# Declared waits of GpSimd operations behind VectorE ones in the paired stage

## The chip, the cores and the metric

The kernel runs on one core of a Trainium2 chip. A core has TensorE (PE in the profile: matrix products into the PSUM banks), VectorE (DVE), ScalarE (ACT), GpSimd (POOL) and SyncE (SP, which issues DMAs). Each works through its own list of instructions in order, and semaphores tie the lists together. The metric is the device time of one execution in microseconds (us), the median of several runs.

## What is computed

Windowed attention with a distance bias, followed by a dense mixture of four experts. All arrays are float32.

```python
# attention: 4 batches, 8 heads, 576 positions, 64 wide; window 128
scores = scale * np.matmul(q, k.transpose(0, 1, 3, 2))
scores = np.where(mask, scores + bias[None], -1000000000.0)   # bias: -slope * distance
attn = np.exp(scores - max); attn = attn / (sum + 1e-09)
attn_out = np.matmul(attn, v)
# experts: x is attn_out as 2304 rows of 512; w1 is 4 x 512 x 1024, w2 is 4 x 1024 x 512
p = domain_probs / (domain_probs.sum(-1, keepdims=True) + 1e-09)
for e in range(E):
    h = np.maximum(x @ w1[e], 0.0)
    out += p[:, e:e + 1] * (h @ w2[e])
```

## The kernel before

Each float32 factor is held as two fp32r numbers, a rounded one (`xh`, `w2h`, `rh`: "high") and the rest (`xl`, `w2l`, `rl`: "low"). A product is made of three matmuls: high x high, high x low, low x high. To split a value is a `cast` (L338 on ScalarE or L340 on VectorE) and then a `minus` (L360 on VectorE or GpSimd), which subtracts the high part from the value.

The 2304 rows stand in seven blocks, the hidden layer in 16 units of 256 columns (four to an expert). For the last blocks, 5 and 6 (384 rows each), units 4 to 15 run two at a time: `pair` (L1329), six pairs, the last 200 us of the kernel. Both layers are done there with seven products of half-size blocks in place of eight, which needs sums and differences of the factors. The first layer is `sevenfold` (matmuls L1236), seven products for each of the two units, called a and b. The second layer is `multiply` (matmuls L1469), products named "12", "22", "11", 1, 2, 3 and 4, each in two parts. Each product is added onto a PSUM bank, and VectorE adds it, weighted with `prob`, into the output tile `acc` (`weighted`, L1488). That is the eviction: a product that adds onto a bank again waits for it. Product 11 and then product 2 use the same two banks.

Products 1 to 4 need four sums S1 to S4 of rectified results, each in two halves of columns (`fi` 0 and 1). `joined` (L1384) and `plus` (L1090) make the raw sums; in the traces they are `w1r` (S1 in one buffer, S2 in the other) and `q` (S3 and S4). `split` (L1396) splits them: S1, S2 and S4 into `xh` and `xl`, S3 into `rh` and `rl`. S4's raw sum is `q<-k,w1r`; S2's is `w1r<-q,k`. Where GpSimd does a `minus` or `plus`, `pieces` (L346) cuts it in two instructions if it has 384 elements or more.

Products 2, 3, 22 and 4 of one pair run among the first-layer products of the next one (the list `rest`): after the first a product comes product 2, part 0, then a, then 2, part 1, and so on. The weights of the pair stage are split already and parked in DRAM; `unparked` (L993) loads them by four DMAs a pair that GpSimd issues. `mixed` (L1021) makes the sums of the second-layer weights (`w2r`, `v`, `acc` to `w2h`, `w2l`, and into `xh`, `xl`).

Nothing is ordered by hand. Each operation is an `Op` with the engines it may run on, a time by which it is due and the keys it reads and writes; `Plan.order` (L88) places one after the other with estimated durations, picks the engine, and the program is emitted in the order of the planned starts. An operation that names VectorE or GpSimd in `port` is kept from overlapping, in the plan, with others that name it. In the program only the data dependencies are enforced, by semaphores; what the plan keeps apart may overlap when the engines run off its times.

Of the kernel before, what the change touches and what calls it, by code (L numbers as in the profile page):

```python
# [11 lines left out]
AF = mybir.ActivationFunctionType  # L12
ALU = mybir.AluOpType
# [7 lines left out]
def f(ap):  # L21
    return ap.bitcast(F32)
# [13 lines left out]


class Op:
    __slots__ = ("n", "engs", "emit", "due", "deps", "outs", "wait", "ready", "bufs", "cold", "start", "end", "eng", "port", "late", "lag")


class Plan:
# [7 lines left out]
    }  # L50

    def __init__(self):
        self.ops, self.last, self.readers, self.places = [], {}, {}, {}

    def op(self, engs, emit, due, reads=(), writes=(), holds=(), cold=None, port=None, late=0.0, lag=0.0):

        o = Op()
        o.n, o.engs, o.emit, o.due = len(self.ops), dict(engs), emit, due
        o.deps, o.outs, o.bufs, o.start = set(), [], [], None


        o.port, o.late, o.lag = (POOL,) if port is None else port, late, lag
        o.cold = 2 * o.engs.get(PE, 0.0) if cold is None else cold
        for key in reads:
            if key in self.last:
                o.deps.add(self.last[key])
        for key in writes:
            if key in self.last:
                o.deps.add(self.last[key])
            o.deps.update(self.readers.get(key, ()))  # L70
        o.deps.discard(o)
        for key in reads:
            self.readers.setdefault(key, []).append(o)
        for key in writes:
            self.last[key] = o
            self.readers[key] = []
        for key in (*reads, *writes, *holds):
            b = key[0] if isinstance(key, tuple) else key
            b = getattr(b, "buf", b)
            if isinstance(b, Buf) and b not in o.bufs:  # L80
                o.bufs.append(b)
                b.uses += 1
        for d in o.deps:
            d.outs.append(o)
        self.ops.append(o)
        return o

    def order(self):  # L88
        at = dict.fromkeys((PE, DVE, ACT, POOL, SP), 0.8)
        queue = {e: [] for e in at}  # L90
        bus = port = 0.0
        landed = [0.0] * FLIGHT
        owner = {tag: [None] * len(p) for tag, p in self.places.items()}

        def push(o):
            o.ready = {e: max((d.end + (EXTRA if d.eng != e or e != PE else 0.0) + self.GAP[d.eng][e] for d in o.deps), default=0.0) + o.late for e in o.engs}
            for e in o.engs:
                queue[e].append(o)

        def slots(o):  # L100

            t, taken = -1.0, []
            for b in o.bufs:
                if b.place is not None:
                    continue
                best = None
                for i, w in enumerate(owner[b.tag]):
                    if (b.tag, i) in taken or (w is not None and w.done < w.uses):
                        continue
                    free = w.free if w is not None else -1.0  # L110
                    if best is None or free < best[0]:
                        best = (free, i)
                if best is None:
                    return None
                t = max(t, best[0])
                taken.append((b.tag, best[1]))
            return t, taken

        for o in self.ops:
            o.wait = len(o.deps)  # L120
            if not o.wait:
                push(o)
        out = []
        while len(out) < len(self.ops):
            best = None
            for e, q in queue.items():
                cands, least = [], None
                for o in q:
                    s = slots(o)
                    if s is None:  # L130
                        continue
                    t = max(at[e], o.ready[e], s[0] + 0.2 if s[1] else 0.0)
                    if e in o.port:
                        t = max(t, port)
                    if e == SP:
                        t = max(t, landed[-FLIGHT])
                    cands.append((t, o, s[1]))
                    least = t if least is None else min(least, t)
                if least is None:
                    continue  # L140
                t, o, taken = min(
                    (c for c in cands if c[0] <= least + SLACK), key=lambda c: (c[1].due, c[1].n)
                )

                key = (t, o.due, o.n)
                if len(o.engs) > 1:
                    end = t + o.engs[e]
                    if any(max(at[x], o.ready[x]) + d < end - 1e-6 for x, d in o.engs.items() if x != e):
                        key = (t + 0.3, o.due, o.n)
                        alt = [c for c in cands if len(c[1].engs) == 1 and c[0] <= least + SLACK]  # L150
                        if alt:
                            t, o, taken = min(alt, key=lambda c: (c[1].due, c[1].n))
                            key = (t, o.due, o.n)
                if best is None or key < best[0]:
                    best = (key, t, e, o, taken)
            assert best is not None, "the plan is stuck"
            _, t, e, o, taken = best
            for x in o.engs:
                queue[x].remove(o)
            o.eng, o.start = e, t  # L160
            if e == SP:
                at[e] = t + 0.5
                bus = max(bus, t + 1.2) + o.engs[e] / DBW
                o.end = bus + 0.85
                landed.append(o.end)
            else:
                o.end = t + (o.cold if e == PE and t < WARM else o.engs[e])
                at[e] = o.end
                if e in o.port:
                    port = o.end  # L170
                o.end += o.lag
            new = [b for b in o.bufs if b.place is None]
            for b, (tag, i) in zip(new, taken):
                owner[tag][i] = b
                b.place = self.places[tag][i]
            for b in o.bufs:
                b.done += 1
                b.free = max(b.free, o.end)
            for x in o.outs:
                x.wait -= 1  # L180
                if not x.wait:
                    push(x)
            out.append(o)
        return sorted(out, key=lambda o: (o.start, o.n))


DBW = 2.4e5
# [2 lines left out]
PLAIN = 4.0  # L190
FLIGHT = 9
SLACK = 0.1
EXTRA = 0.03
LATE_S = 1.79
LATE_T = 1.48
# [49 lines left out]
def attention_moe(  # L245
# [87 lines left out]
    def cast(o, i, n, due, reads, writes, sbuf=True):  # L333


        def emit(e):
            if e == ACT:
                nc.scalar.activation(o(), i(), AF.Copy)  # L338
            else:
                nc.vector.tensor_copy(o(), i())  # L340

        plan.op(
            {ACT: act(n) + (0.035 if sbuf else 0.0), DVE: dve2(n) if sbuf else dve(n)}, emit, due, reads, writes, port=(DVE,) if sbuf else ()
# [8 lines left out]
        at_ = (slice(None),) * axis  # L352
        return [[x[(*at_, slice(i * m, i * m + m))] for x in aps] for i in range(2)]

    def minus(o, a, b, n, due, reads, writes, gp=True):


        def emit(e):
            for x, y, z in pieces(e, n, o(), a(), b()):
                by[e].tensor_tensor(out=x, in0=y, in1=f(z), op=ALU.subtract)  # L360

        engs = {DVE: dve(n), POOL: pooled(n)} if gp else {DVE: dve(n)}
        plan.op(engs, emit, due, reads, writes, port=(DVE, POOL) if gp else ())

# [719 lines left out]

    def plus(o, a, b, n, due, reads, writes, op=ALU.add):
        def emit(e):
            for x, y, z in pieces(e, n, o(), a(), b()):
                by[e].tensor_tensor(out=x, in0=y, in1=z, op=op)  # L1090

        plan.op({DVE: dve(n), POOL: pooled(n)}, emit, due, reads, writes, port=(DVE, POOL))

# [234 lines left out]

    def pair(l0, l1, due, between):  # L1329

        w0 = wst[l0]
        nbs = joint[l0]
        n = BLOCKS[nbs[0]][1]
# [57 lines left out]
        def halves(name, fi, src, keys, d, sbuf, free=()):  # L1391
            h, lo, hk, lk = R[name, fi]
            relu(h, src, [*keys, *free], hk, d)
            joined(lo, src, h, ALU.subtract, [*keys, hk], lk, d, sbuf)

        def split(i, fi):  # L1396
            h, lo, hk, lk = S[i, fi]
            r_, rk = s_raw(i, fi), s_key(i, fi)
            n0 = len(plan.ops)
            cast(h, r_, n, ready[i], [rk], [hk])  # L1400
            minus(lo, r_, h, n, ready[i], [rk, hk], [lk], i > 2)
            if i < 3:
                after_group(n0)

# [12 lines left out]
        def result1(src, keys, fi, b):  # L1417
# [9 lines left out]
            if len(hold) == 1 and (b == 1) == (fi == 0):  # L1427
# [2 lines left out]
                joined(s_raw(3, fi), src, raw(a21, fi), sub, [*keys, key(a21, fi)], s_key(3, fi), d, False)  # L1430
                plus(s_raw(2, fi), s_raw(3, fi), raw(a22, fi), n, ready[2] - 0.5, [key(a22, fi), s_key(3, fi)], [s_key(2, fi)], sub)
                plus(s_raw(4, fi), raw(a12, fi), s_raw(2, fi), n, ready[4] - 0.5, [key(a12, fi), s_key(2, fi)], [s_key(4, fi)])
                split(3, fi)
                if fi:
                    split(2, 0)
                    split(2, 1)

        spare = Buf("av")
        s0, at0, _ = sevenfold(l0, due, result0, Part(spare, lambda t: t.place[0], 0))
# [248 lines left out]
    outs = []  # L1688
# [37 lines left out]
            outs = [] if l in pairs else [(l, b, i) for b in (nb if l in joint else [nb]) for i in range(BLOCKS[b][1] // P)]  # L1726

    with tc.manual_schedule():
        for o in plan.order():
            o.emit(o.eng)  # L1730


MARGIN = 15.32
# [65 lines left out]
```

## Time and profile before

| | us |
|---|---|
| median of 3 runs | 911.28 (911.26 to 913.27) |
| profiled execution | 911.12 |
| its span, first to last instruction | 909.1 |
| TensorE busy | 883.8 (97%) |
| VectorE busy | 739.5 (81%) |
| ScalarE busy | 474.6 (52%) |
| GpSimd busy | 462.0 (51%) |
| mean granted clock of TensorE | 0.991 |

The profile comes from one execution, and its times are counted from the start of the span. An engine's busy time holds no waiting for semaphores, but an instruction that has begun and is held up counts in full. In a timeline a bracket gives the idle time of the engine before the instruction, and who released it. Matmuls overlap with the one before: a row's duration is longer than the distance to the next.

### The profile page before, as it was taken

The numbers are of one execution on the slowest core, as the hardware profiler recorded it, in microseconds if no ns is written. First come the engines' busy times: TensorE is split into PE (matmuls) and PEld (weight loads), VectorE is DVE, ScalarE is ACT, GpSimd is POOL, SyncE is SP. The second block draws the span as 40 slices with busy tenths as digits, with TensorE's granted clock in tenths as the row PEclk, the third lists the DMA queues.
The fourth block names the chain that finished last, engine by engine and source line by source line (L and its number), as shares of the span: only waits on it lengthen the run. The fifth ranks groups of instructions, "written<-read, shape, count | busy, mean of one in ns | idle before, by whom it ended". The sixth has DMA issues, their size and how long they took to land.

```text
span 909.1 us, 15674 instructions
## 1 busy us (share of the span) xinstructions
PE 883.8 (97%) x5466; PEld 816.2 (90%) x5466; DVE 739.5 (81%) x1605; ACT 474.6 (52%) x1221; POOL 462.0 (51%) x595
## 2 busy tenths in 40 slices
PE   8999999999999999999999999999999898998997
PEld 5899999999999999999998989899998898998997
DVE  6989879888887889886998878778665879879877
ACT  6877456565677678663443534334242533543542
POOL 4787555556457678763672213218314415535524
PEclk9999999999999999999999999999999999999999
DMA  7766554242445456432366464642333533533602
GB/s 239 228 199 194 170 169 134 86 153 85 136 164 157 141 179 217 139 120 65 128 242 245 163 218 148 215 150 76 110 96 137 186 105 112 201 105 111 203 1 70
DMA packets 47999, 136.19 MB, mean 150 GB/s; under 512 B 4656, under 2 KB 19760, under 8 KB 44848
## 3 DMA queue, kind: packets, MB, share of 16 engines
q1 hardware_dynamic: 43696, 113.17, 37.7%
q0 software_dynamic: 4224, 22.02, 7.2%
q8 instruction: 43, 0.70, 0.3%
q14 instruction: 36, 0.29, 0.1%
HBM read 106.86 MB, written 28.31 MB: 149 GB/s over the span
## 4 chain that ended last, share of the span: by engine, by line
PE 84%; DVE 10%; DMA 2%; ACT 2%; issue 1%; SPq 1%; DVEq 0%; ACTq 0%
PE b L1564 29%; PE b L1158 19%; PE b L1236 18%; PE b L1469 8%; PE av L819 4%; PE b L609 3%; DVE acc L1488 2%; PE b L746 2%; DMA w2r<-in_w 1%; DVE acc L1582 1%; PE av L1469 1%; DVE xl L360 1%; DVE w2l L360 1%; PE av L1236 1%; DMA q<-in_q 1%
## 5 line engine op out<-in xcount | busy, mean ns | idle before, releaser
L1158 PE MATMUL b<-xh,w 128*128 128x256 f32 (+1 forms) x928 | 205.2, 296 | 1.0 <-DVE xh L340 1.0
L1158 PEld LDWEIGHTS b<-xh,w 128*128 128x128 f32 x928 | 156.5, 190 | 3.3 <-DVE xh L340 1.2
L1582 DVE SCALAR_TENSOR_TENSOR acc<-b,prob,acc 128x512 f32<-128x512 f32 x150 | 111.6, 745 | 36.4 <-PE b L1564 35.5
L1564 PE MATMUL b<-w2h,rh 128*128 128x512 f32 x342 | 135.7, 397 | 0.0
L1158 PE MATMUL b<-xl,w 128*128 128x256 f32 (+1 forms) x464 | 135.4, 292 | 0.1
L1564 PE MATMUL b<-w2l,rh 128*128 128x512 f32 x342 | 134.6, 394 | 0.0
L1564 PE MATMUL b<-w2h,rl 128*128 128x512 f32 x342 | 134.4, 393 | 0.0
L782 POOL TENSOR_SCALAR_AFFINE_SELECT pt<-s 128x512 fp32r<-128x512 f32 x120 | 77.3, 669 | 74.5 <-DVE s L360 61.4
L1158 PEld LDWEIGHTS b<-xl,w 128*128 128x128 f32 x464 | 88.0, 190 | 2.4 <-DVE xl L360 0.3
L1564 PEld LDWEIGHTS b<-w2h,rl 128*128 128x128 f32 x342 | 64.2, 188 | 14.7 <-DVE rl L1186 0.4
L690 ACT ACTIVATE s<-s,t 128x128 f32<-128x128 f32 x128 | 50.4, 395 | 50.9 <-DVE t L672 50.3
L360 DVE TENSOR_TENSOR w2l<-w2r,w2h 128x512 fp32r<-128x512 f32 x85 | 76.6, 924 | 0.4 <-ACT w2h L338 0.4
L1179 ACT ACTIVATE rh<-b 128x256 fp32r<-128x256 f32 (+1 forms) x116 | 45.5, 393 | 57.5 <-PE b L1158 55.5
L360 POOL TENSOR_TENSOR w<-w1r,w 128x256 fp32r<-128x256 f32 x74 | 64.5, 896 | 19.9 <-ACT w L338 12.6
L1564 PEld LDWEIGHTS b<-w2h,rh 128*128 128x128 f32 x342 | 64.5, 189 | 8.2
L1249 ACT ACTIVATE s<-b 128x384 f32<-128x384 f32 x81 | 39.6, 489 | 61.7 <-PE b L1236 61.5
L1564 PEld LDWEIGHTS b<-w2l,rh 128*128 128x128 f32 x342 | 64.5, 189 | 7.9
L1186 DVE SCALAR_TENSOR_TENSOR rl<-b,rh 128x256 fp32r<-128x256 f32 (+1 forms) x116 | 51.2, 441 | 25.0 <-ACT rh L1179 24.3
L360 POOL TENSOR_TENSOR w2l<-w2r,w2h 128x256 fp32r<-128x256 f32 x46 | 39.0, 868 | 51.4 <-ACT w2h L338 35.7
L1488 DVE SCALAR_TENSOR_TENSOR acc<-b,prob,acc 128x256 f32<-128x256 f32 x108 | 46.6, 474 | 12.7 <-PE b L1469 12.4
L1236 PE MATMUL b<-xh,w 128*128 128x384 f32 x192 | 56.9, 337 | 0.0
L338 ACT ACTIVATE w2h<-w2r 128x512 fp32r<-128x512 f32 x95 | 56.1, 619 | 1.3 <-PE b L1564 1.1
(223 smaller groups left out, 2415.2 us busy)
## 6 DMA issues: line engine op xcount, KB each, us to landing
w2r<-in_w SPq DMA_DIRECT2D x60, 512.0 KB, 3.6
w1r<-in_w SPq DMA_DIRECT2D x48, 512.0 KB, 4.5
parked<-w SPq DMA_DIRECT2D x12, 1024.0 KB, 5.5
w<-parked POOLq DMA_DIRECT2D x12, 1024.0 KB, 6.0
q<-in_q SPq DMA_DIRECT2D x16, 384.0 KB, 3.4
k<-in_k SPq DMA_DIRECT2D x12, 512.0 KB, 4.5
k<-in_k SPq DMA_DIRECT2D x12, 384.0 KB, 4.4
parked<-pt SPq DMA_DIRECT2D x6, 768.0 KB, 3.3
```

What stands on the lines that cost most here:

```text
L338: nc.scalar.activation(o(), i(), AF.Copy)
L360: by[e].tensor_tensor(out=x, in0=y, in1=f(z), op=ALU.subtract)
L690: return lambda e: nc.scalar.activation(sv()[:, h, -m:], sv()[:, h, -m:], AF.Exp, bias=t[:, h : h + 1], scale=-1.0, accum_out=t[:, 2 + h : ...
L782: return lambda e: nc.gpsimd.affine_select(out=pt[:, :, :, c0 + own * P : c0 + own * P + P], in_=hl(), pattern=[[0, 4], [1, P] if own else ...
L1158: nc.tensor.matmul(bk[:, :n], a[0][:, kt, fs], b[:, kt, cols], start=kt == 0 and i == 0, stop=kt == KT - 1 and i == 2,)
L1179: lambda e: nc.scalar.activation(h[:, :n], bk[:, :n], AF.Relu),
L1186: lambda e: nc.vector.scalar_tensor_tensor(out=lo[:, :n], in0=bk[:, :n], scalar=0.0, in1=f(h[:, :n]), op0=ALU.max, op1=ALU.subtract,),
L1236: nc.tensor.matmul(bank[:, :n], x(k), y(k), start=new and k == 0 and i == 0, stop=k == 1 and i == 2, skip_group_check=True,)
L1469: nc.tensor.matmul(bank[bk][part]()[:, cs], a()[:, ns], b()[:, fi, :], start=new and i != 1 and fi == 0 and j == 0, stop=fi == 1 and j == ...
L1488: nc.vector.scalar_tensor_tensor(out=ac[:, ds], in0=bank[bk][part]()[:, cs], scalar=prob[:, nt, e_ : e_ + 1], in1=ac[:, ds], op0=ALU.mult, ...
L1564: nc.tensor.matmul(bk[:, cs], a[:, ns], b[1][:, fi, cs], start=half != 1 and fi == 0 and j == 0, stop=half != 0 and fi == 1 and j == 2, sk ...
L1582: nc.vector.scalar_tensor_tensor(out=o, in0=i_, scalar=p, in1=o, op0=ALU.mult, op1=ALU.add)
```

## The change

Three things. `Op` gets a list `after` of operations that it must follow whatever the data say. `Plan.order`, once all is placed, goes through the operations of the paired stage (from number `strict` on) in the order of their planned starts; a GpSimd operation on the port that starts less than `HOLD` = 3 us behind the end of the last VectorE one on the port gets that one into `after`, each VectorE one at most once. When the program is emitted, each entry that is on another engine becomes a declared dependency, hence a semaphore wait: 32 of them. And in `pair` the splits of S2 and S3 are called by turns (S2 half 0, S2 half 1, S3 half 0, S3 half 1), with the subtraction of each S3 half after that of the S2 half; this is an edge for the planner, too.

```diff
@@ class Plan
+        o.after, o.made = list(after), None
+        o.deps.update(after)
         o.deps.discard(o)
@@ order
-        return sorted(out, key=lambda o: (o.start, o.n))
+        out = sorted(out, key=lambda o: (o.start, o.n))
+        held = None
+        for o in out:
+            if o.eng == DVE and DVE in o.port:
+                held = o
+            elif o.eng == POOL and POOL in o.port and held is not None and o.n >= self.strict and held.end > o.start - HOLD:
+                o.after.append(held)
+                o.deps.add(held)
+                held = None
+        return out
...
+HOLD = 3.0
@@ cast, minus, plus: emit returns the instructions it made, as a list; minus takes after=()
...
@@ pair
+        plan.strict = min(plan.strict, len(plan.ops))
...
+        first_ = {}
+
         def split(i, fi):
             h, lo, hk, lk = S[i, fi]
             r_, rk = s_raw(i, fi), s_key(i, fi)
             n0 = len(plan.ops)
             cast(h, r_, n, ready[i], [rk], [hk])
-            minus(lo, r_, h, n, ready[i], [rk, hk], [lk], i > 2)
+            first_[i, fi] = minus(lo, r_, h, n, ready[i], [rk, hk], [lk], i > 2, [first_[2, fi]] if i == 3 else ())
...
-                split(3, fi)
                 if fi:
-                    split(2, 0)
-                    split(2, 1)
+                    for i in (2, 3):
+                        split(i, 0)
+                        split(i, 1)
@@ emitting
+        behind = mybir.DependencyInfo(mybir.DependencyClass.Sync, mybir.DependencyReason.DATA)
         for o in plan.order():
-            o.emit(o.eng)
+            o.made = o.emit(o.eng)
+            for d in o.after:
+                if d.eng != o.eng and isinstance(o.made, list) and isinstance(d.made, list):
+                    tc.add_manual_dep(o.made[0].ins, d.made[-1].ins.name, behind, reason="port")
```

In the built program the lists of TensorE, ScalarE and SyncE hold the same instructions in the same order as before. Lines of the changed file lie 10 to 20 further down (`minus` L370, `plus` L1102, `joined` L1398, the evictions L1504, `unparked` L1010).

GpSimd in the second pair, from the last of the four weight loads on (`rl1`, `rl3` are S3's two low halves, `q0_63` is S4's raw sum, `w1r1_93<-q1_64,k1_66` is S2's second half; the brackets name the semaphores waited for, DVE being VectorE's). Before:

```order
L999 DMA w11_97<-parked90_138 128x2048 [waits DMASW7_49,PE_49]
L1090 TENSOR_TENSOR w1r1_93<-q1_64,k1_66 128x192 [waits DVE_49]
L1090 TENSOR_TENSOR w1r1_93<-q1_64,k1_66 128x192
L360 TENSOR_TENSOR rl1_107<-q1_64,rh1_103 128x192 [waits Activation_49]
L360 TENSOR_TENSOR rl1_107<-q1_64,rh1_103 128x192 [waits PE_49]
L360 TENSOR_TENSOR rl3_109<-q1_64,rh3_105 128x192 [waits Activation_49]
L360 TENSOR_TENSOR rl3_109<-q1_64,rh3_105 128x192 [waits PE_49]
L360 TENSOR_TENSOR w2l0_100<-w2r1_95,w2h0_98 128x256 [waits DMAHW7_49,Activation_49]
L360 TENSOR_TENSOR w2l0_100<-w2r1_95,w2h0_98 128x256
```

The same place now, down to the next weight split:

```order
L1010 DMA w11_97<-parked90_138 128x2048 [waits DMASW7_49,PE_49]
L1102 TENSOR_TENSOR w1r1_93<-q1_64,k1_66 128x192 [waits DVE_49]
L1102 TENSOR_TENSOR w1r1_93<-q1_64,k1_66 128x192
L370 TENSOR_TENSOR rl1_107<-q1_64,rh1_103 128x192 [waits DVE_49,Activation_49]
L370 TENSOR_TENSOR rl1_107<-q1_64,rh1_103 128x192 [waits PE_49,Pool_49]
L1102 TENSOR_TENSOR q0_63<-k0_65,w1r1_93 128x192 [waits Pool_49] x2
L370 TENSOR_TENSOR rl3_109<-q1_64,rh3_105 128x192 [waits DVE_49]
L370 TENSOR_TENSOR rl3_109<-q1_64,rh3_105 128x192 [waits PE_49]
L1102 TENSOR_TENSOR v0_67<-v1_68,w2r1_95 128x256 [waits DMAHW7_49,DVE_49]
L1102 TENSOR_TENSOR v0_67<-v1_68,w2r1_95 128x256
L370 TENSOR_TENSOR w2l1_101<-v0_67,w2h1_99 128x256 [waits DVE_49,PE_49,Activation_49]
```

The first piece of `rl1` waits for VectorE's first `xl1_91<-w1r1_93` below, `rl3` for the second, and `w2l1_101` for VectorE's own `w2l1_101`; a `q0_63` has come between, and `w2l0_100` is gone to VectorE.

VectorE at the same place, from the first of the two low halves of S2 on (`acc` rows are evictions). Before:

```order
L360 TENSOR_TENSOR xl1_91<-w1r1_93,xh1_89 128x384
L1488 SCALAR_TENSOR_TENSOR acc5_115<-b2_122,prob_165,acc5_115 128x256
L1488 SCALAR_TENSOR_TENSOR acc0_110<-b2_122,prob_165,acc0_110 128x256
L1488 SCALAR_TENSOR_TENSOR acc1_111<-b5_125,prob_165,acc1_111 128x256
L360 TENSOR_TENSOR xl1_91<-w1r1_93,xh1_89 128x384
L1488 SCALAR_TENSOR_TENSOR acc9_119<-b0_120,prob_165,acc9_119 128x256
L1488 SCALAR_TENSOR_TENSOR acc7_117<-b0_120,prob_165,acc7_117 128x256
L1488 SCALAR_TENSOR_TENSOR acc2_112<-b3_123,prob_165,acc2_112 128x256
L1090 TENSOR_TENSOR q0_63<-k0_65,w1r1_93 128x384 x2
L1090 TENSOR_TENSOR acc3_113<-w2r1_95,w2r0_94 128x512
L1090 TENSOR_TENSOR v1_68<-w2r0_94 128x512
L1488 SCALAR_TENSOR_TENSOR acc9_119<-b0_120,prob_165,acc9_119 128x256
```

Now, from the second of them on:

```order
L370 TENSOR_TENSOR xl1_91<-w1r1_93,xh1_89 128x384
L1504 SCALAR_TENSOR_TENSOR acc9_119<-b0_120,prob_165,acc9_119 128x256
L1504 SCALAR_TENSOR_TENSOR acc7_117<-b0_120,prob_165,acc7_117 128x256
L1504 SCALAR_TENSOR_TENSOR acc2_112<-b3_123,prob_165,acc2_112 128x256
L370 TENSOR_TENSOR w2l0_100<-w2r1_95,w2h0_98 128x2x256
L1102 TENSOR_TENSOR q0_63<-k0_65,w1r1_93 128x384
L1102 TENSOR_TENSOR acc3_113<-w2r1_95,w2r0_94 128x512
L1102 TENSOR_TENSOR v1_68<-w2r0_94 128x512
L1504 SCALAR_TENSOR_TENSOR acc9_119<-b0_120,prob_165,acc9_119 128x256
```

The rows ahead of the second low half are the same; behind the evictions a `w2l0_100` has taken the place of one `q0_63`. Pairs 3 to 5 read alike.

GpSimd in the first pair, between the last weight load and the next pair's work. Before:

```order
L999 DMA w11_97<-parked70_134 128x2048 [waits DMASW3_49,PE_49]
L360 TENSOR_TENSOR rl1_107<-q1_64,rh1_103 128x192 [waits Activation_49]
L360 TENSOR_TENSOR rl1_107<-q1_64,rh1_103 128x192 [waits PE_49]
L360 TENSOR_TENSOR rl2_108<-q1_64,rh2_104 128x192 [waits Activation_49]
L360 TENSOR_TENSOR rl2_108<-q1_64,rh2_104 128x192
L1090 TENSOR_TENSOR q0_63<-k1_66,w1r1_93 128x192 [waits Pool_49] x2
```

And now:

```order
L1010 DMA w11_97<-parked70_134 128x2048 [waits DMASW3_49,PE_49]
L1102 TENSOR_TENSOR q0_63<-k1_66,w1r1_93 128x192 [waits DVE_49,Pool_49]
L1102 TENSOR_TENSOR q0_63<-k1_66,w1r1_93 128x192 [waits Pool_49]
L370 TENSOR_TENSOR rl1_107<-q1_64,rh1_103 128x192 [waits DVE_49]
L370 TENSOR_TENSOR rl1_107<-q1_64,rh1_103 128x192 [waits PE_49]
L370 TENSOR_TENSOR w2l0_100<-w2r0_94,w2h0_98 128x256 [waits DVE_49,Activation_49]
L370 TENSOR_TENSOR w2l0_100<-w2r0_94,w2h0_98 128x256
```

`q0_63` has moved ahead, and waits for VectorE's `w1r1_93<-q1_64,k0_65`; `rl2_108` is VectorE's, right behind its second `xl1_91<-w1r1_93`, and `w2l0_100`, which was VectorE's, waits for it. In the sixth pair only the last `rl3` and `q0` of GpSimd change places.

## Rows read from the trace of the kernel before

**Rows 1.** The page's first part: busy time, share of the span, instructions.

```profile
PE 883.8 (97%) x5466; PEld 816.2 (90%) x5466; DVE 739.5 (81%) x1605; ACT 474.6 (52%) x1221; POOL 462.0 (51%) x595
```

**Rows 2.** Timeline, TensorE's stops: start, us, instruction, [idle before <-releaser].

```profile
692.48 1.34 PE L1236 MATMUL b<-pt,w 128*128 128x384 f32 x6 [0.93 <-DVE x L1316]
...
728.40 0.36 PE L1469 MATMUL b<-w2h,xh 128*128 128x256 f32 x1 [2.44 <-DVE acc L1488]
762.52 0.36 PE L1469 MATMUL b<-w2h,xh 128*128 128x256 f32 x1 [2.67 <-DVE acc L1488]
...
864.84 0.35 PE L1469 MATMUL b<-w2h,xh 128*128 128x256 f32 x1 [2.68 <-DVE acc L1488]
895.96 0.36 PE L1469 MATMUL b<-w2h,xh 128*128 128x256 f32 x1 [0.74 <-DVE acc L1488]
```

**Rows 3.** Timeline, TensorE around its third long stop.

```profile
793.45 0.33 PE L1236 MATMUL b<-xl,w 128*128 128x384 f32 x1
793.62 0.34 PE L1236 MATMUL b<-xh,w 128*128 128x384 f32 x1
796.62 0.36 PE L1469 MATMUL b<-w2h,xh 128*128 128x256 f32 x1 [2.66 <-DVE acc L1488]
...
800.71 0.28 PE L1469 MATMUL b<-w2h,xh 128*128 128x256 f32 x1
...
802.46 0.28 PE L1469 MATMUL b<-xh,rh 128*128 128x256 f32 x1
...
804.94 0.28 PE L1469 MATMUL b<-xh,rh 128*128 128x256 f32 x1
```

**Rows 4.** Windows: us, busy of PE, PEld, DVE, ACT, POOL, PEclk, DMA, GB/s.

```profile
600.00:700.00 100.00, 99.07 (x495) 88.94 (x494) 69.89 (x112) 35.04 (x67) 40.24 (x43) 1.00 0.34 116
...
796.00:798.00 2.00, 1.38 (x9) 1.41 (x10) 2.00 (x6) 0.00 (x0) 0.00 (x0) 0.81 0.00 0
798.00:800.00 2.00, 2.00 (x9) 2.00 (x9) 1.88 (x4) 0.63 (x1) 0.85 (x2) 0.50 0.03 8
...
895.96:909.10 13.14, 9.12 (x72) 8.71 (x72) 6.52 (x16) 0.52 (x1) 1.19 (x3) 1.00 0.36 121
```

**Rows 5.** Timeline, VectorE across the third stop.

```profile
789.79 4.25 DVE L360 TENSOR_TENSOR xl<-w1r,xh 128x384 fp32r<-128x384 f32 x1
793.97 1.26 DVE L1488 SCALAR_TENSOR_TENSOR acc<-b,prob,acc 128x256 f32<-128x256 f32 x3
...
795.61 1.25 DVE L1488 SCALAR_TENSOR_TENSOR acc<-b,prob,acc 128x256 f32<-128x256 f32 x3
796.79 1.01 DVE L1090 TENSOR_TENSOR q<-k,w1r 128x384 f32<-128x384 f32 x2
797.72 0.68 DVE L1090 TENSOR_TENSOR acc<-w2r,w2r 128x512 f32<-128x512 f32 x1
```

**Rows 6.** Timeline, GpSimd at the same place.

```profile
788.23 0.57 POOL L999 DMA_DIRECT2D w<-parked  x1
788.81 1.18 POOL L1090 TENSOR_TENSOR w1r<-q,k 128x192 f32<-128x192 f32 x2
789.96 2.27 POOL L360 TENSOR_TENSOR rl<-q,rh 128x192 fp32r<-128x192 f32 x4
792.21 1.42 POOL L360 TENSOR_TENSOR w2l<-w2r,w2h 128x256 fp32r<-128x256 f32 x2
```

**Rows 7.** Timeline, TensorE: last matmul of product 11, part 0, third stop.

```profile
791.90 0.28 PE L1469 MATMUL b<-w2h,xl 128*128 128x256 f32 x1
```

**Rows 8.** Timelines of VectorE and GpSimd in the sixth pair.

```profile
894.13 0.90 DVE L360 TENSOR_TENSOR xl<-w1r,xh 128x384 fp32r<-128x384 f32 x1
...
893.44 2.60 POOL L360 TENSOR_TENSOR rl<-q,rh 128x192 fp32r<-128x192 f32 x4
```

**Rows 9.** Timelines of VectorE and GpSimd in the first pair.

```profile
721.99 2.77 DVE L1090 TENSOR_TENSOR w1r<-q,k 128x384 f32<-128x384 f32 x1
...
723.19 1.15 POOL L1090 TENSOR_TENSOR q<-k,w1r 128x192 f32<-128x192 f32 x2
```

More of the change, by code (lines that the diff above doesn't have):

```diff
@@ L38 @@
 class Op:
-    __slots__ = ("n", "engs", "emit", "due", "deps", "outs", "wait", "ready", "bufs", "cold", "start", "end", "eng", "port", "late", "lag")
+    __slots__ = ("n", "engs", "emit", "due", "deps", "outs", "wait", "ready", "bufs", "cold", "start", "end", "eng", "port", "late", "lag", "after", "made")
 class Plan:
@@ L52, in __init__, with op @@
     def __init__(self):
-        self.ops, self.last, self.readers, self.places = [], {}, {}, {}
-    def op(self, engs, emit, due, reads=(), writes=(), holds=(), cold=None, port=None, late=0.0, lag=0.0):
+        self.ops, self.last, self.readers, self.places, self.strict = [], {}, {}, {}, 1e9
+    def op(self, engs, emit, due, reads=(), writes=(), holds=(), cold=None, port=None, late=0.0, lag=0.0, after=()):
         o = Op()
@@ L337, in emit @@
             if e == ACT:
-                nc.scalar.activation(o(), i(), AF.Copy)
-            else:
-                nc.vector.tensor_copy(o(), i())
+                return [nc.scalar.activation(o(), i(), AF.Copy)]
+            return [nc.vector.tensor_copy(o(), i())]
         plan.op(
@@ L353, in pieces, with minus @@
         return [[x[(*at_, slice(i * m, i * m + m))] for x in aps] for i in range(2)]
-    def minus(o, a, b, n, due, reads, writes, gp=True):
+    def minus(o, a, b, n, due, reads, writes, gp=True, after=()):
         def emit(e):
-            for x, y, z in pieces(e, n, o(), a(), b()):
-                by[e].tensor_tensor(out=x, in0=y, in1=f(z), op=ALU.subtract)
+            return [
+                by[e].tensor_tensor(out=x, in0=y, in1=f(z), op=ALU.subtract) for x, y, z in pieces(e, n, o(), a(), b())
+            ]
         engs = {DVE: dve(n), POOL: pooled(n)} if gp else {DVE: dve(n)}
-        plan.op(engs, emit, due, reads, writes, port=(DVE, POOL) if gp else ())
+        return plan.op(engs, emit, due, reads, writes, port=(DVE, POOL) if gp else (), after=after)
     a, b = EARLY
@@ L1088, in emit @@
         def emit(e):
+            made = []
             for x, y, z in pieces(e, n, o(), a(), b()):
-                by[e].tensor_tensor(out=x, in0=y, in1=z, op=op)
+                made.append(by[e].tensor_tensor(out=x, in0=y, in1=z, op=op))
+            return made
         plan.op({DVE: dve(n), POOL: pooled(n)}, emit, due, reads, writes, port=(DVE, POOL))
```

## The prediction

> **What bounds the kernel now.** I read the page's first part, then TensorE's own stops over the whole span in the timeline, then the timelines of VectorE and GpSimd across one stop, then the windows for the clock. TensorE is busy 97% of the span [rows 1], so time is won only where it stands still or runs slowly. Its long stops all lie in the paired stage, the last 200 us: one in each of the first five of its six pairs, at 728.40 (2.44 us) and then four alike, 762.52 to 864.84, of 2.66 to 2.68 us [rows 2]. Each ends with VectorE's evictions at L1488, and each stands at the same matmul: product 2, which adds onto the bank that product 11 has left and that VectorE has to empty first.
>
> What a stop costs is read at the third one [rows 3]. The last two matmuls before it start 0.17 us apart, so the next could have started at 793.79; it started at 796.62, 2.83 us late. [...] The next 18 matmuls (12 of 256 columns, 6 of 384) take 4.09 us, from 796.62 to 800.71; an equal group from 802.46 to 804.94 takes 2.48 us [rows 3]. So the slow stretch costs 1.61 us more, and the whole stop 4.44 us. Shorter stops have no such tail: 0.93 us at 692.48 and 0.74 us at 895.96 [rows 2] lie in windows whose clock is 1.00 [rows 4].
>
> Why VectorE is late: its subtraction xl <- w1r, xh (low half of the second sum, SBUF in and out) is issued at 789.79 and takes 4.25 us, until 794.04 [rows 5]. GpSimd runs without a gap from 788.81 to 793.63 in eight pieces [rows 6], and VectorE ends 0.41 us behind the last of them: it waits for the whole run, past seven piece ends. The evictions queue behind it: three at 793.97, three more, the ones that TensorE wants, at 795.61 [rows 5]. The second of these starts 0.39 us behind the first and takes 0.47, so it ends near 796.47, and TensorE starts 0.15 us later.
>
> **The change, part by part.** *The wait in front of rl1.* GpSimd's first subtraction of sum 3 now waits for that xl. The run then breaks at 789.99, where the w1r pieces end [rows 6]; VectorE takes 0.41 and is through at 790.40 instead of 794.04. Three evictions (1.26 us) follow until 791.6, and the second xl (other half of the columns) is issued at 791.5.
>
> *What stands in its way there.* Behind the wait GpSimd runs rl1 and then q0 (formerly on VectorE), four pieces, and they have no wait between them. Four pieces took 2.27 us [rows 6]; from about 790.5 they reach 792.8. This decides between two cases. Either VectorE gets in at the end of the piece that is running, as it did in the last pair (issued at 894.13, through after 0.90 us, while four rl pieces stretched to 2.60 us instead of 2.27 [rows 8, 6]), or only at the end of the run, as in pairs 1 to 5. I take the first: there, as after this wait, no DMA issue stands right in front of the run, while at 789.79 and 721.99 one did (788.23 in [rows 6]). Then xl is through at about 792.1, the matmuls of product 11 end at 791.90 + 0.28 = 792.18 [rows 7], its first two evictions end at 793.1, and TensorE, which asks at 793.79, does not stop. In the second case xl ends at 793.2, the evictions at 794.0, TensorE starts at 794.2: a stop of 0.4 us.
>
> [...]
>
> *Sum for pairs 2 to 5:* 4 x 4.44 = 17.8 us.
>
> *Pair 1.* Its stop has another victim: VectorE's w1r <- q, k, issued at 721.99, takes 2.77 us, until GpSimd's q pieces end at 723.19 + 1.15 [rows 9]. TensorE could have started at 728.40 - 2.44 - 0.17 = 725.79, so the stop costs 2.61 + 1.61 = 4.22. Now q0 waits for w1r, rl1 for xl, and rl2 goes to VectorE. w1r (0.54, as an unhindered one of the two at 796.79 [rows 5]) and xl end at 723.0, three evictions at 724.2, the second xl meets q0 and rl1 and ends at 725.1 (by the second case 725.7), rl2 0.5 later, two evictions 0.86 later; TensorE starts at 726.5 (727.1). A stop of 0.7 (1.3) us is left, and I take it without slow clock, since 0.93 us had none. Gain 3.5 (2.9).
>
> *What moves to VectorE and away from it.* In pairs 2 to 5 the w2l split of 128x512 goes from GpSimd (1.42 us [rows 6]) to VectorE (0.60 from start to start, 797.72 to the next of its kind; 0.68 long [rows 5]), and one q0 the other way (0.47): VectorE has 0.13 us more. These stand ahead of the evictions of product 2: from 793.1 w2l, q0 and two more run until 795.4, just when product 2 is done (793.79 + 1.6), and its two evictions end at 796.3. The next product on this bank starts at 793.79 + (802.46 - 796.62 - 1.61) = 798.02 [rows 3]: 1.6 us to spare, or 0.2 if the chain meets one further GpSimd run of 1.4. That is what is late next. rl3 ends near 794.4 instead of 792.23 [rows 6]; its user is that product at 798.02, 3.6 us later. Pair 6 changes only the order of rl3 and the last q0: its 0.74 stays.
>
> **The sum.** 17.8 + 3.5 = 21.2 us off 911.1 (the profiled execution: span 909.1 and 2.0 around it) gives 889.9; the median shown is 0.2 above that execution, so 890.1.
>
> **Rivals.** *Only at the end of the run:* 4 x 0.4 more in pairs 2 to 5, 0.6 in pair 1: 892.2. For it: five stops of before behaved so. Against: the last pair.
>
> *A new stop takes the old one's place:* the chain with w2l in front of product 2's evictions is late, by GpSimd pieces that each VectorE operation meets. A stop of 1 us in each of pairs 2 to 5 leaves 4 x 3.44 + 3.5, so 894; with the slow clock behind each, 4 x 1.83 + 3.5, so 900.5. For it: VectorE has few gaps here. Against: 1.6 us to spare. Range of this case 894 to 901.
>
> *The waits do nothing:* if VectorE's 4.25 us came from something other than GpSimd, all five stops stay: 911. Against: its end 0.41 us behind GpSimd's last piece, and 2.77 us in pair 1 with the same 0.42.
>
> *Slower:* GpSimd becomes late. rl3 now waits for the second xl, and behind rl3 stand all other GpSimd operations of the pair, four DMA issues among them. If rl3 ends d us later than the 794.4 above, product 3 stops for d - 3.6, with 1.61 on top for the clock. Against the 4.44 of before that loses in pairs 2 to 5 from d = 6.4 on, and against pair 1's 3.5 as well from d = 7.3; at d = 8 the time is 911.1 + 4 x 1.6 - 3.5 = 914. That would need three runs of four pieces (2.27 each) ahead of rl3; the rows show one.
>
> **How the numbers follow.** First case 0.50 (890.1), end of the run 0.27 (892.2), new stop 0.15 (894 to 901), no effect 0.05 (911), slower 0.03 (914). The likeliest gives the time. Its own range is 888.5 (pair 1's rest and the stop of 0.74 go too) to 891.5; with the second case and the cheaper half of the third the range is 888.5 to 896.0, with some 0.15 outside. What tells a change from none here is 0.3%, 2.7 us: faster 0.93, within it 0.04, slower 0.03.
>
> **What would show it.** Right: the xl that is issued behind the evictions of the av banks takes under 1 us in all pairs instead of 4.25; no stop over 1 us in pairs 2 to 5, and stop-to-stop distance 29.7 us instead of 34.1; the granted clock 1.00 in every window of the stage; pair 1 with 0.5 to 1.3 us left. The second case shows as a second xl of about 1.7 us and stops of 0.2 to 0.4. Wrong: an xl still over 2 us, a stop at product 3, 22 or 4 or at rl3, or clock windows at 0.50 behind stops that have shrunk under 2 us.

## The result, and the profile after

The changed kernel took 890.29 us (median of 6 runs, 890.06 to 892.85), the kernel before, beside it, 912.61 (911.26 to 913.27). The ratio is 0.9766, with a 95% interval of 0.9751 to 0.9781. The forecast was 890.1, within 888.5 to 896.0. The profiled span is 888.4 us against 909.1.

The page's first part, as in [rows 1]:

```profile
PE 874.7 (98%) x5466; PEld 808.6 (91%) x5466; DVE 725.2 (82%) x1605; ACT 474.3 (53%) x1221; POOL 461.5 (52%) x595
```

TensorE's stops in the paired stage, as in [rows 2]; the list names every one over 0.3 us:

```profile
692.71 1.31 PE L1249 MATMUL b<-pt,w 128*128 128x384 f32 x6 [1.74 <-DVE x L1329]
716.53 1.31 PE L1249 MATMUL b<-pt,w 128*128 128x384 f32 x6 [0.65 <-DVE x L1329]
721.16 0.39 PE L1485 MATMUL b<-w2h,xl 128*128 128x256 f32 x1 [0.57 <-DVE xl L370]
727.03 0.36 PE L1485 MATMUL b<-w2h,xh 128*128 128x256 f32 x1 [0.85 <-DVE acc L1504]
875.26 0.35 PE L1485 MATMUL b<-w2h,xh 128*128 128x256 f32 x1 [0.74 <-DVE acc L1504]
```

The four stops of 2.66 to 2.68 us of pairs 2 to 5 are gone, and pair 1's has shrunk from 2.44 to 0.85. The matmul that stood last before the third of them and the one that had to wait (start, duration):

```profile
786.25 0.33 PE L1249 MATMUL b<-xh,w 128*128 128x384 f32 x1
786.43 0.28 PE L1485 MATMUL b<-w2h,xh 128*128 128x256 f32 x1
```

They start 0.18 us apart; in [rows 3] it was 3.00. The clock at this place and in the stretch that holds pair 1's stop, columns as in [rows 4]:

```profile
720.00:740.00 20.00, 18.58 (x134) 18.09 (x134) 19.29 (x42) 8.60 (x18) 7.51 (x12) 1.00 0.26 83
...
780.00:800.00 20.00, 20.00 (x149) 20.00 (x148) 18.83 (x40) 9.05 (x20) 13.17 (x20) 1.00 0.33 116
```

TensorE is busy for all 20 us, at 1.00; behind the stop of before it was 0.81 and then 0.50 [rows 4]. VectorE there, as in [rows 5]:

```profile
782.42 0.61 DVE L370 TENSOR_TENSOR xl<-w1r,xh 128x384 fp32r<-128x384 f32 x1
782.95 1.25 DVE L1504 SCALAR_TENSOR_TENSOR acc<-b,prob,acc 128x256 f32<-128x256 f32 x3
784.13 0.62 DVE L370 TENSOR_TENSOR xl<-w1r,xh 128x384 fp32r<-128x384 f32 x1
784.86 1.27 DVE L1504 SCALAR_TENSOR_TENSOR acc<-b,prob,acc 128x256 f32<-128x256 f32 x3
786.05 0.84 DVE L370 TENSOR_TENSOR w2l<-w2r,w2h 128x512 fp32r<-128x512 f32 x1
786.81 0.95 DVE L1102 TENSOR_TENSOR q<-k,w1r 128x384 f32<-128x384 f32 x1
...
788.89 1.40 DVE L1504 SCALAR_TENSOR_TENSOR acc<-b,prob,acc 128x256 f32<-128x256 f32 x3
```

And GpSimd, as in [rows 6]:

```profile
780.85 0.57 POOL L1010 DMA_DIRECT2D w<-parked  x1
781.44 1.17 POOL L1102 TENSOR_TENSOR w1r<-q,k 128x192 f32<-128x192 f32 x2
783.17 1.17 POOL L370 TENSOR_TENSOR rl<-q,rh 128x192 fp32r<-128x192 f32 x2 [0.56 <-ACT xh L350]
784.30 1.47 POOL L1102 TENSOR_TENSOR q<-k,w1r 128x192 f32<-128x192 f32 x2
```

The first xl is issued at 782.42 and through at 783.03, where it was 4.25 us before: GpSimd's w1r pieces end at 782.61, and it needs 0.42 from there. The pause of 0.56 us in front of rl is the declared wait. The profile puts it down to a cast of ScalarE, but rl starts 0.14 us behind the end of xl; a releaser is inferred, and where a wait is new, the end times have to be read too. The second xl, issued at 784.13 while rl and q run without a gap, is through after 0.62 and pushes a piece of q back (1.47 for two where rl took 1.17).

### The profile page after: what moved, and what is told of

It is laid out like the page before. It is cut to its first block, busy times and chain, and to the rows that moved or that the text cites. A ratio compares the mean times of both kernels' runs of the same rounds, so it can differ in the third digit from the quotient of the medians.

```text
span 888.4 us, 15675 instructions
## 1 busy us (share of the span) xinstructions
PE 874.7 (98%) x5466; PEld 808.6 (91%) x5466; DVE 725.2 (82%) x1605; ACT 474.3 (53%) x1221; POOL 461.5 (52%) x595
## 4 chain that ended last, share of the span: by engine, by line
PE 85%; DVE 9%; DMA 2%; ACT 2%; issue 1%; SPq 1%; POOL 0%; DVEq 0%; ACTq 0%
PE b L1580 30%; PE b L1171 19%; PE b L1249 18%; PE b L1485 7%; PE av L830 4%; PE b L620 3%; PE b L757 2%; DMA w2r<-in_w 1%; DVE acc L1598 1%; DVE acc L1504 1%; PE av L1485 1%; DVE xl L370 1%; PE av L1249 1%; DVE w2l L370 1%; SPq L343 1%
## 5 line engine op out<-in xcount | busy, mean ns | idle before, releaser
L370 DVE TENSOR_TENSOR w2l<-w2r,w2h 128x512 fp32r<-128x512 f32 x88 | 77.0, 898 | 0.4 <-ACT w2h L350 0.4
L370 POOL TENSOR_TENSOR w<-w1r,w 128x256 fp32r<-128x256 f32 x74 | 64.4, 894 | 19.9 <-ACT w L350 12.6
L370 POOL TENSOR_TENSOR w2l<-w2r,w2h 128x256 fp32r<-128x256 f32 x40 | 34.7, 887 | 51.7 <-ACT w2h L350 35.4
L1504 DVE SCALAR_TENSOR_TENSOR acc<-b,prob,acc 128x256 f32<-128x256 f32 x108 | 46.7, 475 | 6.2 <-PE b L1485 5.6
```

Source lines behind the costliest of these rows:

```text
L1504: nc.vector.scalar_tensor_tensor(out=ac[:, ds], in0=bank[bk][part]()[:, cs], scalar=prob[:, nt, e_ : e_ + 1], in1=ac[:, ds], op0=ALU.mult, ...
```

## The experiments

Each was timed beside the kernel before on the same chip. Medians in us, ratio to before with its interval:

| kernel | median | ratio | longest xl in pairs 2 to 5, where over 1 us |
|---|---|---|---|
| e1, waits in the old order | 908.89 | 0.997 (0.9958 to 0.9983) | 4.25 |
| e2, new order, no waits | 908.25 | 0.9962 (0.9946 to 0.9977) | 3.98 |
| e3, loads issued by SyncE | 889.22 | 0.9756 (0.9736 to 0.9775) | none |
| e4, only the 11 waits at rl | 889.95 | 0.9763 (0.9746 to 0.978) | none |
| e5, e3 with a fill in front | 891.12 | 0.9782 (0.9767 to 0.9796) | none |
| e6, e3 with a small issue in front | 907.39 | 0.996 (0.9945 to 0.9975) | 4.25 |
| e7, only the fourth load by SyncE | 891.04 | 0.9783 (0.9766 to 0.98) | none |
| e8, e4 and e3 together | 889.50 | 0.9761 (0.9746 to 0.9776) | none |
| f1, the changed kernel again | 891.26 | 0.9773 (0.9755 to 0.979) | none |
| f2, e3 again | 889.14 | 0.975 (0.9735 to 0.9766) | none |

**Which part does it.** e1 takes the order of the splits back and keeps the rule of the planner:

```diff
-            first_[i, fi] = minus(lo, r_, h, n, ready[i], [rk, hk], [lk], i > 2, [first_[2, fi]] if i == 3 else ())
+            first_[i, fi] = minus(lo, r_, h, n, ready[i], [rk, hk], [lk], i > 2)
...
+                split(3, fi)
                 if fi:
-                    for i in (2, 3):
-                        split(i, 0)
-                        split(i, 1)
+                    split(2, 0)
+                    split(2, 1)
```

> The changed kernel without the new order of the splits: every list of instructions is that of the kernel before, and only the planner's own rule adds waits. In the built program GpSimd gets 8 new waits: two early in pair 1's weight sums, two in pair 1 (rl1 behind VectorE's w1r, q0 behind the second xl), and one each in pairs 2 to 5, at w2l1, which stands behind the run that locks VectorE out; none before rl1 there. Theory (the run in front of xl must be broken at rl1): the four stops of 2.66 us in pairs 2 to 5 stay, with their slow clock; only pair 1 gains, 2.5 to 3.5 us: 908 to 909. Rival (any wait for VectorE in the stage, or the spacing that the waits bring, does it): the stops go, 890 to 893.

Measured: 908.89. The four stops stayed (2.70, 2.66, 2.68, 2.68 us), and pair 1's fell to 1.00. Pair 1 has a new wait inside its run; in pairs 2 to 5 the rule puts none there. e2 is the other half:

```diff
-                if d.eng != o.eng and isinstance(o.made, list) and isinstance(d.made, list):
+                if False:
```

> The changed kernel with all its lists of instructions as they are, but none of the declared waits is emitted. Theory: behind the weight load GpSimd then runs w1r, rl1, q0 and rl3 without a wait, 8 pieces of about 4.6 us together; xl is locked out to their end as before, and in pairs 2 to 5 the stops stay at 2.3 to 2.6 us with the slow clock behind each: 908 to 911. Rival (the order does it: w2l has gone to VectorE and q0 has come in its place): stops under 1 us, 890 to 895.

Measured: 908.25. The four stops stayed at 2.38 to 2.43 us, pair 1's at 1.89. One xl of VectorE and the run of GpSimd, the same instructions in the same order as after, without the wait:

```profile
787.21 3.96 DVE L370 TENSOR_TENSOR xl<-w1r,xh 128x384 fp32r<-128x384 f32 x1
```

```profile
785.64 0.57 POOL L1010 DMA_DIRECT2D w<-parked  x1
786.22 1.17 POOL L1102 TENSOR_TENSOR w1r<-q,k 128x192 f32<-128x192 f32 x2
787.35 1.16 POOL L370 TENSOR_TENSOR rl<-q,rh 128x192 fp32r<-128x192 f32 x2
788.48 1.16 POOL L1102 TENSOR_TENSOR q<-k,w1r 128x192 f32<-128x192 f32 x2
789.60 1.15 POOL L370 TENSOR_TENSOR rl<-q,rh 128x192 fp32r<-128x192 f32 x2
```

The xl ends at 791.17, 0.42 us behind the last piece: locked out to the end of the run, again. So the order alone is worth 3.8 us and the rule alone 3.1, and neither removes the four stops: in the old order the rule puts no wait inside the run. A wait named there in the old order was not tried. e4 asks which waits:

```diff
-HOLD = 3.0
+HOLD = -1e9
```

> The changed kernel with the planner's rule off (HOLD far below zero), so that only the waits named in the code are left: each low half of sum 3 on GpSimd behind VectorE's low half of sum 2. The lists are those of the changed kernel; 11 of its 19 effective waits are left (rl1 in pairs 1 to 6, the second rl in pairs 2 to 6), and those at v, q0, w2l0 and w2l1 are gone. Theory: these 11 do all the work in pairs 2 to 5, and the early ones at v cost 0.2 us at the stop before pair 1: 889.5 to 890.5, if pair 1 holds; there q0 stands in front of rl1 without a wait and can lock out w1r again, which would leave a stop of up to 2 us in pair 1: up to 892.5. Rival (the w2l1 waits matter too): a stop of 0.5 to 2 us at product 2, part 1, or at product 3 in pairs 2 to 5: 893 to 900.

Measured: 889.95. Of the 32 declared waits 19 add a wait on VectorE in the built program, and the 11 in front of an rl do all that can be measured; which of these 11 could go was not tried. Pair 1 held too: a stop of 0.64.

**Why the run locks VectorE out.** The prediction leaned on one observation: a GpSimd DMA issue stood in front of the runs that locked VectorE out, and none in front of the others. e3 takes the issues from GpSimd and changes the kernel before in nothing else (`f` views the tile as float32; the same bytes move):

```diff
-                lambda e, o=o, i=i: nc.gpsimd.dma_start(out=o(), in_=i[:]),
+                lambda e, o=o, i=i: nc.sync.dma_start(out=f(o()), in_=i[:]),
```

> The kernel before, with the four loads of parked weights of each pair issued by SyncE in place of GpSimd; nothing else moves, and no wait is declared. Theory A (a run of GpSimd pieces keeps VectorE out past its piece ends only where a DMA issue of GpSimd stands right in front of it): xl gets in at the next piece end, takes 0.6 to 1.2 us in place of 4.25, and the stops of pairs 1 to 5 shrink to under 0.5 us: 889 to 893. Rival B (any run without a gap keeps VectorE out, whatever stands in front): xl stays at 3 to 4.3 us and the time at 906 to 911. In both, SyncE could hold up its own later loads; that would show as TensorE waiting for a DMA.

Measured: 889.22, with no declared wait at all. TensorE waited for no DMA there, but pair 1 kept a stop of 1.04 us where under 0.5 was expected: VectorE's operations still meet GpSimd's pieces (the xl of e3 took 0.55 to 0.95). VectorE's two xl and GpSimd's run in one pair:

```profile
781.43 0.92 DVE L360 TENSOR_TENSOR xl<-w1r,xh 128x384 fp32r<-128x384 f32 x1
...
783.45 0.91 DVE L360 TENSOR_TENSOR xl<-w1r,xh 128x384 fp32r<-128x384 f32 x1
```

```profile
778.15 1.76 POOL L360 TENSOR_TENSOR xl<-w2r,xh 128x256 fp32r<-128x256 f32 x2
779.87 1.50 POOL L1090 TENSOR_TENSOR w1r<-q,k 128x192 f32<-128x192 f32 x2
781.34 2.60 POOL L360 TENSOR_TENSOR rl<-q,rh 128x192 fp32r<-128x192 f32 x4
783.90 1.75 POOL L360 TENSOR_TENSOR w2l<-w2r,w2h 128x256 fp32r<-128x256 f32 x2
```

The run is longer than that of [rows 6], without a gap from 778.15 to 785.65, and VectorE gets in at a piece end each time; GpSimd's pieces stretch (2.60 for four rl, 2.27 before). The length of the run is not it. Two kernels put something back where the fourth issue stood, e5 a fill and e6 a small DMA:

```diff
+        issued[0] += 1
+        if issued[0] % 4 == 0:
+            nc.gpsimd.memset(f(o[:, 0, 0:512]), 0.0)                     # e5 alone
+            nc.gpsimd.dma_start(out=o[:, 0, 0:16], in_=i[:, 0, 0:16])    # e6 alone
+        nc.sync.dma_start(out=f(o), in_=i[:])
```

> The kernel of e3 (the kernel before, parked weights loaded by SyncE) with one instruction put where the fourth of GpSimd's four DMA issues of each pair stood: GpSimd fills 128x512 of the tile with zeros, and SyncE's load then overwrites them. So the run of GpSimd pieces in front of VectorE's xl again stands directly behind another GpSimd instruction, but that is no DMA issue. Theory (it takes a DMA issue): xl stays under 1.3 us and the time at 889 to 893. Rival (any instruction directly in front, or a longer run without a gap, does it): xl 3 to 4.3 us, 905 to 911.

> The kernel of e3 with a small DMA put where the fourth of GpSimd's four DMA issues of each pair stood: GpSimd issues the load of 16 of the 2048 columns, and SyncE's load then brings the whole tile. Theory (the issue itself sets the state in which the run behind it keeps VectorE out, whatever it moves): the long xl of 3 to 4.3 us and the stops of 2 to 2.7 us in pairs 2 to 5 are back: 902 to 911. Rival (what counts is the transfer of 1 MB that runs beside the pieces): xl under 1.3 us, 889 to 893.

Measured: 891.12 and 907.39. In e5 the fill at the place of the issue takes 0.53 us, about what the issue took (0.57), and VectorE gets in (0.54 and 0.91). In e6 the lockout is back to the digit:

```profile
784.31 0.57 POOL L998 DMA_DIRECT2D w<-parked  x1
784.90 1.17 POOL L1098 TENSOR_TENSOR w1r<-q,k 128x192 f32<-128x192 f32 x2
786.04 2.29 POOL L360 TENSOR_TENSOR rl<-q,rh 128x192 fp32r<-128x192 f32 x4
788.30 1.42 POOL L360 TENSOR_TENSOR w2l<-w2r,w2h 128x256 fp32r<-128x256 f32 x2
```

```profile
785.89 4.25 DVE L360 TENSOR_TENSOR xl<-w1r,xh 128x384 fp32r<-128x384 f32 x1
```

So it is the issue and not the megabyte that it moves, and a fill of nearly the same length in its place does not do it (0.53 us; xl 0.54 and 0.91). The first pair of e6 shows the other half, an issue with a pause behind it (GpSimd's rows, then VectorE's):

```profile
718.92 0.57 POOL L998 DMA_DIRECT2D w<-parked  x1
720.20 2.92 POOL L360 TENSOR_TENSOR rl<-q,rh 128x192 fp32r<-128x192 f32 x4 [0.70 <-ACT rh L338]
```

```profile
720.61 0.60 DVE L1098 TENSOR_TENSOR w1r<-q,k 128x384 f32<-128x384 f32 x1
721.14 0.95 DVE L360 TENSOR_TENSOR xl<-w1r,xh 128x384 fp32r<-128x384 f32 x1
```

Here GpSimd stood for 0.70 us between the issue and the run, and the run locks nobody out, where that of [rows 9] held w1r for 2.77. The two differ in the pause, and the small issue did lock VectorE out in pairs 2 to 5 (4.25); so it seems to be the pause of 0.70 that kept w1r at 0.60 here. It is one case, which came about by itself. In pairs 2 to 5 the declared wait gives such a pause (0.56 us), there behind the two pieces of w1r. e7 moves the fourth issue of the kernel before alone:

```diff
-                lambda e, o=o, i=i: nc.gpsimd.dma_start(out=o(), in_=i[:]),
+                lambda e, o=o, i=i: sent(o(), i),
...
+        issued[0] += 1
+        if issued[0] % 4 == 0:
+            nc.sync.dma_start(out=f(o), in_=i[:])
+        else:
+            nc.gpsimd.dma_start(out=o, in_=i[:])
```

> The kernel before with only the fourth of the four loads of each pair issued by SyncE, the other three by GpSimd as before. Theory (only the issue directly in front of the run counts): as e3, 889 to 893. Rival (an issue earlier in the pair has the same effect on the run, as long as GpSimd has not been idle for long): stops of over 1 us stay in pairs 2 to 5, 897 to 911.

Measured: 891.04, no long xl: the one issue directly in front is enough to explain all four stops, and with the three earlier ones of a pair left in place the xl at that run took 0.92 and 0.90, as in e3.

**Both remedies.** e8 is e4 with the edit of e3:

> The kernel of e4 (changed order, only the waits named in the code) with all parked weights loaded by SyncE: both remedies together. If the two remove the same stops, nothing is left for the second: 888.5 to 889.9. If the locked-out time that is left at the first pair's stop (0.6 to 1.0 us) is still of that kind, up to 0.6 less: 888.3. If GpSimd, relieved of its issues, meets VectorE elsewhere: 890 to 892.

Measured: 889.50, between e3 and e4: they remove the same stops. f1 and f2 compare the change with e3 on one chip:

> The changed kernel once more, beside the kernel of e3 on the same chip, to compare the two remedies: 890.0 to 890.5. What it has more than e3 is the early waits of pair 1 and the splits of w2l on VectorE.

> The kernel of e3 once more: 889.0 to 889.5 if the 1.1 us between it and the changed kernel are real (GpSimd relieved of its issues and of the early waits); the same as the changed kernel within 0.3 us if they came from the chip or the day.

Measured: 891.26 and 889.14. f1 missed its range. Its stops stand at the places of those above, but in f1 the clock falls behind the one ahead of pair 1. The windows behind that stop, in the first profile of the changed kernel (1.74 us long) and in f1's (1.84):

```profile
694.00:696.00 2.00, 2.00 (x14) 2.00 (x13) 1.62 (x3) 1.12 (x3) 1.78 (x3) 1.00 1.00 329
```

```profile
694.00:696.00 2.00, 2.00 (x9) 2.00 (x8) 1.67 (x4) 1.10 (x3) 1.83 (x3) 0.52 0.88 276
```

With 1.61 us for such a stretch, that is most of the 1.9 us between the two spans (888.4 and 890.3). The result's own six runs part in the same way: four lie at 890.06 to 890.31 with a mean clock of 1.000, two at 892.24 and 892.85 with 0.997, as f1's profile has. e3 is the faster remedy, by 2.1 us beside the changed kernel on one chip and by 1.1 between the first runs of each, which were not timed side by side; and it needs no waits.

## Why the prediction was right

*Cause and place.* Right: the four stops went with the lockout of xl, and e2 and e3 show that the wait, or its cause, decides and not the order. One reading was off by one: of the eight pieces of [rows 6] the first was over at about 789.4, before xl was issued at 789.79, so xl passed six ends and came in behind the seventh.

*The size, pairs 2 to 5.* From pair 1's stop to pair 6's it was 895.96 - 728.40 = 167.56 us [rows 2] and is 875.26 - 727.03 = 148.23. Of the 19.33 between, 1.61 is put down to the slow clock behind pair 1's stop (0.74, 0.50 and 0.90 in the three windows of 2 us from 728 on; the 1.61 is that of the third stop); 17.7 are left, against 17.8 in the sum. In pairs 2 to 5 the price of 4.44 for a stop with its slow clock held.

*How near the time came.* 890.29 against 890.1 is closer than the sum was. 17.8 and 3.5 make 21.3, not the 21.2 of the sum; it took 21.2 off the span, and 20.7 came. The 0.2 added for the median did not (median 890.29, profiled execution 890.31), and 1.9 us stood outside the span, not 2.0. That these made up for most of the 0.5 is luck.

*First case or second.* The first, as taken: the second xl took 0.62 us, not some 1.7, and none of the stops of 0.2 to 0.4 us came. The two evictions that TensorE wants ended at about 785.74, 0.69 us before product 2 began at 786.43; forecast were 793.1 and 793.79, the same distance. The reason given (no issue in front of that run) was an inference from two kinds of places; e3, e5, e6 and e7 have tested it.

*Pair 1.* Forecast 3.5 with a stop of 0.7; measured from the stop at 716 to this one, 716.32 to 728.40 before and 716.53 to 727.03 now, 1.58 less, and 1.61 of slow clock behind it: 3.2, with a stop of 0.85. The second xl there took the 0.9 that was counted. The rl behind it met GpSimd's pieces, too, and took 0.88 from its start to the next instead of 0.5; and the 0.15 from the end of the second eviction to TensorE's start, which the prediction had read at the third stop, was left out of this chain.

*What is late next.* The order of things was right, the margin too wide. Product 2's first two evictions ended at 788.89 + 0.39 + 0.47 = 789.75, 3.3 us behind product 2's start, where 2.5 was forecast. Of the difference 0.3 is the third of the three evictions at 784.86, which stands in front of w2l and which the chain left out (w2l began at 786.05, not at 785.74); 0.16 and 0.40 came as w2l and q met GpSimd's pieces (0.84 and 0.95 in the rows of VectorE above, 0.76 and 0.87 from start to start). Product 3 started at 790.65 without a stop, 0.9 us behind those evictions; in the forecast (798.02 and 796.3) it was 1.7. This rival was nearer than its 0.15 looked.

*What the sum left out.* Two effects before pair 1 nearly cancel. The stop at 692 grew from 0.93 to 1.74. It is 1.74, 1.84 and 2.15 us in the three profiles with the two early waits at v (after, f1, e1), and 0.81 to 1.58 in the eight without them besides before (0.93). So these waits seem to cost some tenths there, and they bring the stop to where the clock fell in one of the three profiles (f1, 1.84 us, to 0.52); no pair of kernels that differ in these two waits alone was timed. Against it, this execution was 0.48 us ahead by the stop at 487 (486.82, 487.30 before). The two leave 0.33, of which 0.1 was won back on the way: at 716 it is 0.21 behind. 17.7 + 3.2 - 0.2 = 20.7 us is the whole difference of the spans.

## What to carry to other kernels

Where a VectorE operation takes several times its usual length (here 4.25 us where 0.54 to 0.96 is usual), look at what stands in front of the run that GpSimd has at that time: a DMA issue with no pause behind it was the cause here. Give the issue to SyncE first, which cost one line, kept TensorE waiting for no DMA here and won 1 to 2 us more than 32 declared waits; if it has to stay, a pause in GpSimd's run in front of the place where VectorE's operation is due was enough here (0.70 us right behind the issue in e6, 0.56 two pieces further on in the changed kernel). A wait is worth only what its place is worth: in e1 those of pairs 2 to 5 stand behind the run, and all four stops stayed.

## What the runs showed of the hardware

*VectorE does not always get in at the end of a GpSimd piece.* In a run of GpSimd pieces that follows its own DMA issue without a pause, VectorE's subtraction passed six piece ends and was through 0.41 to 0.42 us behind the seventh, the last of the run (before at 789.79, e2 at 787.21, e6 at 785.89; e1 has an xl of 4.25 us as well). One such meeting is left in the changed kernel, where it stops nothing for long: a w1r of VectorE at 716.86 takes 1.78 us, to 0.43 behind the two pieces that follow the issue at 716.18; before and e4 have it too (1.78 at 716.65 and 716.67). Where no issue stood in front, the subtraction came in at the next end or so (0.54 to 0.96 us for all 36 of these xl, two in each of six pairs, in e3, e5 and e7). Why the issue does this, and how short a pause ends it (0.56 and 0.70 us did), is open; no shorter one was tried.

*The clock does not answer to the length of a stop alone.* Behind two stops of e2 that are alike, 2.39 us at 827.61 and 2.39 at 859.91, the granted clock stayed at 1.00 and fell to 0.50 (us, busy of PE, PEld, DVE, ACT, POOL, PEclk, DMA, GB/s):

```profile
829.00:831.00 2.00, 2.00 (x16) 2.00 (x15) 1.92 (x4) 0.84 (x2) 0.79 (x2) 1.00 0.00 0
...
861.00:863.00 2.00, 2.00 (x10) 2.00 (x10) 1.70 (x4) 0.54 (x1) 0.49 (x1) 0.50 0.00 0
```

A stop of 1.84 us was followed by a fall in f1 (to 0.52), while those of 2.15 (e1), 1.89 (e2, at 727.60) and 1.74 (after) were not (1.00). The 1.61 us for a slow stretch held in the sum where the clock fell. It fell behind all five stops of 2.44 to 2.68 us of before (to 0.50) and all four of 2.66 to 2.70 of e1 (to 0.52 to 0.56), and behind three of the four of 2.38 to 2.43 of e2 (to 0.50 to 0.55); for a stop of 1.8 to 2.4 us it has to be given a chance, and the spread between runs of one kernel (e2: 905.98 to 910.29) is of the size of one to three such stretches.
